# Four plain experts instead of five in the first token group, and six half-units of forms made inside the block-product stage

## The chip, the cores and the metric

One core of a Trainium2 chip runs the whole program. TensorE (PE; PEld is its weight load) multiplies, VectorE (DVE), ScalarE (ACT) and GpSimd (POOL) do the elementwise work, SyncE (SP) issues the DMAs. The metric is device microseconds of one execution.

## The reference

Three layers follow each other. Local attention: 4 batches, 8 heads, 576 positions, head size 64, causal with a window of 64. Then a feed-forward layer (below "first mixture stage") with an ELU on 2304 tokens, 512 to 2048 to 512. Then a dense mixture of eight experts, each 512 to 1024 to 512 with a ReLU, weighted by a matrix P that eight Sinkhorn rounds make from gate logits:

```
h = x @ w_in;  g = where(h > 0, h, exp(min(h, 0)) - 1);  x = g @ w_out
P = exp(x @ w_gate - max);  8 times: P /= P.sum(1); P /= P.sum(0); P *= N / E
for e in range(8):
    h = maximum(x @ w1[e], 0.0)
    out += P[:, e:e + 1] * (h @ w2[e])
```

Nearly all the time is in the matrix products. Each float32 operand is held as a rounded high part and the rest, and a product is three matmuls (high x high, high x rest, rest x high).

## The kernel before

The tokens of the experts are cut into three groups of 768 (NG2 = 3). The experts are computed in two ways.

**Plain** (e_in, e_out): the first group is done as two blocks of 512 and 256 tokens. A unit of this stage is half an expert, four chunks of 128 hidden columns; a chunk is 12 matmuls into a hidden tile (lines 886 to 888), ReLU and split, then matmuls into the outputs (lines 904 to 906). Its weights lie in SBUF as "forms". Experts 0 to KP-1 = 4 are done so for the first group.

**Block product** (l1, l2): an expert on 768 tokens is cut 2 x 2 in each dimension, and seven products take the place of eight. A period (g, e, pp) is half an expert on group g. It has 14 calls of l1 (six matmuls each on 384 columns, line 1080), two per step of the outer loop, and seven calls of l2 (line 1225 in the first group, 18 matmuls on 256 columns; line 1160 in the others, 12 on 384). l2 runs eight steps behind l1, so the first eight steps of the stage have one call of l2 among them. In l1 the accumulator "la" takes four products one on another; between them ACT copies its state out ("a", "u", "v", line 1100), and TensorE must not write it again before. DVE forms c11, c22, c21 and the sums s1 to s4; ACT and DVE or POOL split them into the hidden operands h (lines 1053, 1058, 1062). Experts KP to 7 of the first group and all experts of the other two groups are done so: 6 + 16 + 16 = 38 periods. The weights come from DRAM, where the forms of all eight experts were stored: w1_load puts 256 KB into one of NW1 = 12 buffers, w2_load 512 KB into one of seven. Each w1_load stands 12 calls ahead of its use.

**Forms.** A half-unit is one quarter of an expert's w1 or w2: h = e*8 + p*2 + m, m = 0 for w1 and 1 for w2. Four loads of 128 KB bring it in, POOL makes four sums, ACT rounds the eight pieces (copies), DVE takes the rest (subtractions), and seven pieces of 256 KB go to DRAM. Two pieces of code do it:

- p_tasks, in the last unit of the first mixture stage and through the plain stage, in the order of the list "order" and at the times of a list "due" (12 clocks per plain unit). It has three load buffers, and the forms lie in eight slots, from which the plain stage also uses them.
- q_tasks (lines 771 to 824), for the first N1 half-units of the list "others" (experts 7, 6, ..., KP), in the middle units of the first mixture stage. It has one load buffer "qw", where the sums are made in place, and two form buffers "qf" that go straight to DRAM. It returns ten tasks: load, two empty ones, copies, subtractions with their stores (a store stands on SP behind the subtraction), sums, copies, and so on.

The order on each engine is the order of the code; nothing reorders it. All these DMAs go through SP in that order.

Of the kernel before, what the change touches and what calls it, by code (L numbers as in the profile page):

```python
# [8 lines left out]
F32 = mybir.dt.float32  # L9
R32 = mybir.dt.float32r  # L10
# [8 lines left out]
def kernel(  # L19
# [660 lines left out]

    KP, N1, N3 = 5, 9, 7
    others = [e * 2 * NP + i for e in reversed(range(KP, E)) for i in range(2 * NP)]
    order = [(h, (i + N3) % 2) for i, h in enumerate(others[N1:N1 + N3])]
    NPRE = N3 + 2
    rest = others[N1 + N3:]
    for u in range(2 * KP):
# [1 line left out]
        if u >= 2 and rest:  # L690
            hs.insert(1, (rest.pop(0), hs[3][1]))
        order += hs
    assert sorted([h for h, _ in order] + others[:N1]) == list(range(E * NP * 2))
    rws, sws, forms = {}, {}, {}
    pools = {}

# [67 lines left out]

    def q_tasks(h):
        e, p, m = p_at(h)
        st = {}
        pos = ({2: 0, 0: 1, 3: 2, 1: 3}, {0: 0, 2: 1, 3: 2, 1: 3})[m]  # L770
        to = wd1[e][p] if m == 0 else wd2[e][p // 2][:, :, p % 2]
        hf, hd = FF // 2, DM // 2

        def load():
            rw = st["rw"] = pools["pre"].tile([P, 4, HB2], F32, tag="qw", bufs=1, name="qw")
            for (f, d), s in PURE[m].items():
                f0 = f * hf + p * P
                o = rw[:, pos[s]]
                if m == 0:
                    nc.sync.dma_start(  # L780
                        out=o.rearrange("p (c f) -> p c f", c=2),
                        in_=w1[e][d * hd:(d + 1) * hd, f0:f0 + P].rearrange(
                            "(c p) f -> p c f", p=P
                        ),
                    )
                else:
                    nc.sync.dma_start(out=o, in_=w2[e][f0:f0 + P, d * hd:(d + 1) * hd])

        def high(a, n):
            t = st[a] = pools["pre"].tile([P, 2, 2, HB2], R32, tag="qf", bufs=2, name="qf")  # L790
            nc.scalar.activation(t[:, :n, 0, :], st["rw"][:, a % 4:a % 4 + n], AF.Copy)

        def low(a, n):
            t = st[a]
            nc.vector.tensor_tensor(
                out=t[:, :n, 1, :], in0=st["rw"][:, a % 4:a % 4 + n], in1=r(t[:, :n, 0, :]),
                op=ALU.subtract,
            )
            if a >= 4:
                nc.sync.dma_start(out=to[:, a - 1:a + 1], in_=r(t))  # L800
            else:
                for i in range(n):
                    s = [s for s in pos if pos[s] == a + i][0]
                    nc.sync.dma_start(out=to[:, s], in_=r(t[:, i]))

        def sums():
            rw = st["rw"]
            ops = (
                ((0, 2, 0, ALU.add), (2, 1, 2, ALU.subtract), (1, 0, 1, ALU.subtract),
                 (3, 3, 1, ALU.subtract)),  # L810
                ((0, 2, 0, ALU.subtract), (2, 1, 2, ALU.subtract), (1, 0, 1, ALU.subtract),
                 (3, 3, 1, ALU.add)),
            )[m]
            for o, a, b, op in ops:
                nc.gpsimd.tensor_tensor(out=rw[:, o], in0=rw[:, a], in1=rw[:, b], op=op)

        def nothing():
            pass

        return [  # L820
            load, *[nothing] * 2, lambda: high(0, 2), lambda: (low(0, 2), high(3, 1)),
            lambda: low(3, 1), sums, lambda: high(4, 2),
            lambda: (low(4, 2), high(6, 2)), lambda: low(6, 2),
        ]

# [424 lines left out]
    with tc.manual_schedule():  # L1250
# [152 lines left out]
        for s, st in enumerate(steps):  # L1403
# [16 lines left out]
            if (u, su) == (1, 2):  # L1420
                pre_cm, pools["pre"] = pool("pre")
                qtasks = [f for h in others[:N1] for f in q_tasks(h)]
            elif u < NU - 1 and (u, su) > (1, 2):
                for _ in range(min(2 + su % 2, len(qtasks))):
                    qtasks.pop(0)()
            if u == NU - 1:
                if su == 0:
# [3 lines left out]
                if su == 2:  # L1431
                    assert not bg
                    close(wa_cm)
                    close(raw_cm)
                    open_pool("rw", "right")
                    open_pool("A1", "right")
                    for n in range(3):
                        p_load(n)
                    ptasks += [f for n in range(len(order)) for f in p_tasks(n)]
                elif su > 2:  # L1440
                    while ntask < min(5 * NPRE + 3, 3.0 * (su - 2)):
                        ptasks.pop(0)()
                        ntask += 1
            if extra:
# [72 lines left out]
        ps_cm.__exit__(None, None, None)  # L1517
        for nm in ("w2p", "hp", "tp", "pb"):
            P2[nm + "_cm"], P2[nm] = pool(nm)
        ps2_cm, P2["ps2"] = pool("ps2", space=PSUM)  # L1520
        nw2 = 0
        for s in range(NPD * 7 + LAG):
            k, j = divmod(s, 7)
            if k < NPD:
                for z, (p, pi) in enumerate(pairs[j]):
# [3 lines left out]
                    for f in fs:  # L1529
                        f()  # L1530
                    w1_load(s * 2 + z + NW1)
            if s == LAG - 3:
                l2(0, 0)
            elif s > LAG:
# [10 lines left out]
            for k2 in (k, k + 1, k + 2, k + 3):  # L1545
                if k >= 0 and 0 < k2 < NPD and periods[k2][0] != periods[k2 - 1][0]:
                    slot = 7 * (k - k2 + 2) + j
                    if slot == -7:
                        x_load(periods[k2][0])
                    x_plan(slot)  # L1550
                    if slot == 16:
# [43 lines left out]
```

## Time and profile before

| | us |
|---|---|
| median of 3 runs | 1970.4 (1970.08 to 1970.88) |
| profiled execution, its own time | 1974.2 |
| its span, first to last instruction | 1972.4 |
| PE busy | 1954.1 |
| DVE busy | 1494.2 |
| ACT busy | 858.4 |
| POOL busy | 726.1 |

By the timeline the attention and the first mixture stage reach to about 502 us, the plain stage from there to about 847, the block stage from there to the end. Matmuls are pipelined, so a matmul's own duration is longer than the distance to the next; how long a piece of the program takes is read from the distance of two starts. A table of windows gives each engine's busy time in each stretch. The DMA share counts the 16 DMA engines; since packets can overlap in one engine it can exceed 1.

### The profile page before, as it was taken

Reading aid. Unit: us, or ns where it says so; the run is one execution under the profiler, and the core shown is the slowest. Engines: PE = TensorE matmul, PEld = TensorE weight load, DVE = VectorE, ACT = ScalarE, POOL = GpSimd, SP = SyncE. Lnnn points to the kernel's source line nnn. Section 1 sums busy time; section 2 is a strip of 40 time slices with the busy share of each in tenths; the row PEclk is TensorE's granted clock in tenths of the full one; section 3 lists DMA queues with packets and bytes.
Section 4 is the critical chain, followed back from the end, with each engine's and each line's share of the span. In section 5 each row is a group of like instructions: output and inputs, shape, how many; then the busy total and the mean of one; then the engine's idle time right before and its main releaser. Section 6 shows DMA issues by size and latency. Waiting matters only on the chain.

```text
span 1972.4 us, 33582 instructions
## 1 busy us (share of the span) xinstructions
PE 1954.1 (99%) x11856; PEld 1816.9 (92%) x11856; DVE 1494.2 (76%) x2534; ACT 858.4 (44%) x1801; POOL 726.1 (37%) x723
## 2 busy tenths in 40 slices
PE   8999999999999999999999999999999999999999
PEld 6788888898878888899999999999999999999998
DVE  6746676767698656567787888888888888888886
ACT  8875555555543444333343333333334333333332
POOL 5423232332355554342342323323343323333232
PEclk9999999999999999999999999999999999999999
DMA  9851354467699999868878888888887887888884
GB/s 212 165 110 52 100 173 151 154 210 275 213 381 374 374 366 365 314 234 284 263 242 305 260 261 257 255 266 262 291 260 250 270 266 259 260 260 262 238 279 121
DMA packets 307640, 487.84 MB, mean 247 GB/s; under 512 B 79872, under 2 KB 161936, under 8 KB 303632
## 3 DMA queue, kind: packets, MB, share of 16 engines
q1 hardware_dynamic: 306288, 485.39, 76.3%
q8 instruction: 95, 1.56, 0.3%
q14 instruction: 73, 0.60, 0.1%
q10 hardware_dynamic: 1184, 0.30, 0.1%
HBM read 354.44 MB, written 126.95 MB: 244 GB/s over the span
## 4 chain that ended last, share of the span: by engine, by line
PE 90%; DVE 4%; DMA 2%; ACT 2%; SPq 1%; issue 1%; POOL 0%; ACTq 0%; DVEq 0%; POOLq 0%
PE la L1080 15%; PE ob L1160 11%; PE oa L1160 11%; PE lb L1080 11%; PE p L204 3%; PE ac L538 3%; PE p L206 3%; PE ac L540 3%; PE p L205 2%; PE ac L539 2%; PE ac L904 2%; PE ac L905 2%; PE ac L906 2%; PE p L886 2%; PE p L888 2%; PE p L887 2%
## 5 line engine op out<-in xcount | busy, mean ns | idle before, releaser
L1062 POOL TENSOR_TENSOR h<-s,h 128x384 fp32r<-128x384 f32 x304 | 352.6, 1175 | 721.1 <-ACT h L1053 680.2
L1080 PE MATMUL la<-xf,w1f 128*128 128x384 f32 x1824 | 360.0, 335 | 1.9 <-ACT u L1100 1.3
L1080 PEld LDWEIGHTS la<-xf,w1f 128*128 128x128 f32 x1824 | 318.3, 188 | 3.4 <-ACT u L1100 2.1
L1080 PE MATMUL lb<-xf,w1f 128*128 128x384 f32 x1368 | 273.7, 334 | 0.0
L1053 ACT ACTIVATE h<-s 128x384 fp32r<-128x384 f32 x304 | 155.1, 522 | 245.7 <-DVE s L1104 238.4
L1160 PE MATMUL oa<-h,w2f 128*128 128x384 f32 x1344 | 252.2, 334 | 0.0
L1160 PE MATMUL ob<-h,w2f 128*128 128x384 f32 x1344 | 252.0, 334 | 0.2 <-DVE acc L1177 0.2
L1080 PEld LDWEIGHTS lb<-xf,w1f 128*128 128x128 f32 x1368 | 239.9, 188 | 0.0
L1160 PEld LDWEIGHTS ob<-h,w2f 128*128 128x128 f32 x1344 | 234.4, 188 | 0.5 <-DVE acc L1177 0.5
L1160 PEld LDWEIGHTS oa<-h,w2f 128*128 128x128 f32 x1344 | 234.4, 188 | 0.1
L1058 DVE SCALAR_TENSOR_TENSOR h<-c,h 128x384 fp32r<-128x384 f32 x228 | 187.6, 833 | 31.9 <-ACT h L1053 31.2
L1053 ACT ACTIVATE h<-c 128x384 fp32r<-128x384 f32 x228 | 119.7, 525 | 173.7 <-DVE c L1090 162.6
L725 POOL TENSOR_TENSOR sw<-rw 128x256 f32<-128x256 f32 x110 | 101.0, 919 | 204.6 <-DVE f L755 127.8
L1090 DVE TENSOR_TENSOR c<-c,pb 128x384 f32<-128x384 f32 x192 | 144.5, 753 | 6.6
L1177 DVE TENSOR_TENSOR acc<-oa,acc 128x768 f32<-128x768 f32 (+1 forms) x114 | 105.0, 924 | 37.4 <-PE oa L1160 37.4
L1177 DVE TENSOR_TENSOR acc<-ob,acc 128x768 f32<-128x768 f32 (+1 forms) x110 | 101.2, 923 | 37.1 <-PE ob L1160 37.1
L1104 DVE SCALAR_TENSOR_TENSOR s<-c,s 128x384 f32<-128x384 f32 x152 | 108.3, 713 | 12.0 <-DMA out_dram<-ost 1.0
L246 ACT ACTIVATE hh<-p 128x512 fp32r<-128x512 f32 (+1 forms) x80 | 39.2, 490 | 171.9 <-PE p L888 171.8
L247 DVE SCALAR_TENSOR_TENSOR hl<-p,hh 128x512 fp32r<-128x512 f32 (+1 forms) x80 | 44.3, 556 | 88.5 <-ACT hh L246 88.5
L886 PE MATMUL p<-xh,f 128*128 128x512 f32 (+1 forms) x320 | 108.4, 339 | 0.0
L887 PE MATMUL p<-xl,f 128*128 128x512 f32 (+1 forms) x320 | 107.6, 336 | 0.0
L888 PE MATMUL p<-xh,f 128*128 128x512 f32 (+1 forms) x320 | 107.5, 336 | 0.0
(175 smaller groups left out, 3907.3 us busy)
## 6 DMA issues: line engine op xcount, KB each, us to landing
w1f<-wdi SPq DMA_DIRECT2D x532, 256.0 KB, 4.0
w2f<-wdo SPq DMA_DIRECT2D x266, 512.0 KB, 4.4
wdo<-f SPq DMA_DIRECT2D x28, 1024.0 KB, 7.7
rw<-in_moe_w_dram SPq DMA_DIRECT2D x220, 128.0 KB, 4.9
wdi<-f SPq DMA_DIRECT2D x27, 1024.0 KB, 7.1
wdo<-f SPq DMA_DIRECT2D x28, 768.0 KB, 5.6
wdi<-f SPq DMA_DIRECT2D x27, 768.0 KB, 5.0
raw<-in_moe_w_in_dram SPq DMA_DIRECT2D x16, 512.0 KB, 4.3
```

Source lines behind the costliest of these rows:

```text
L725: nc.gpsimd.tensor_tensor(out=sw[:, o], in0=a, in1=b, op=op)
L886: nc.tensor.matmul(p1[:, :n], w[:, s, 0, cs], xh, start=(c == 0), stop=False)
L887: nc.tensor.matmul(p1[:, :n], w[:, s, 0, cs], xl, start=False, stop=False)
L888: nc.tensor.matmul(p1[:, :n], w[:, s, 1, cs], xh, start=False, stop=(c == NCC - 1))
L1053: nc.scalar.activation(h[:, 0], src, AF.Relu if relu else AF.Copy)
L1058: nc.vector.scalar_tensor_tensor(h[:, 1], src, 0.0, r(h[:, 0]), op0=ALU.max, op1=ALU.subtract)
L1062: nc.gpsimd.tensor_tensor(out=h[:, 1], in0=src, in1=r(h[:, 0]), op=ALU.subtract)
L1080: nc.tensor.matmul(o, w[:, a, c, :], x[:, b, c, :], start=first and c == 0 and z == 0, stop=last and c == 1 and z == 2, skip_group_check=True,
L1090: nc.vector.tensor_tensor(out=t, in0=t, in1=pb[g, e][:, i], op=ALU.mult)
L1104: nc.vector.scalar_tensor_tensor(d[nm], d[a], 0.0, d[b], op0=ALU.max, op1=op)
L1160: nc.tensor.matmul(o[:, c], w[:, p, b, c * P:(c + 1) * P], hs[p][:, a, :], start=fresh and p == 0 and z == 0, stop=False, skip_group_check ...
L1177: nc.vector.tensor_tensor(out=a, in0=src, in1=a, op=ALU.add)
```

## The change

KP goes from 5 to 4, so expert 4 is done as a block product in all three groups: eight periods in the first group instead of six, 40 in all. N1 goes from 9 to 11 (half-units by q_tasks in the first mixture stage), N3 from 7 to 9 (by p_tasks in its last unit). Six half-units of expert 7, the list "tail", are taken out of "others" and are made by q_tasks inside the block stage, one task after each l1 call from the first on, with three empty tasks behind the load (11 tasks per half-unit, 66 in all) and with buffers in a new pool "late". That pool is closed before the inputs of the second group are loaded.

```
-    KP, N1, N3 = 5, 9, 7
-    others = [e * 2 * NP + i for e in reversed(range(KP, E)) for i in range(2 * NP)]
+    KP, N1, N3 = 4, 11, 9
+    tail = [(E - 1) * 2 * NP + i for i in (2, 3, 4, 6, 5, 7)]
+    others = [
+        h for e in reversed(range(KP, E)) for h in range(e * 2 * NP, (e + 1) * 2 * NP) if h not in tail
+    ]
...
-    def q_tasks(h):
+    def q_tasks(h, pre="pre", gap=2):
...
-            load, *[nothing] * 2, lambda: high(0, 2), lambda: (low(0, 2), high(3, 1)),
+            load, *[nothing] * gap, lambda: high(0, 2), lambda: (low(0, 2), high(3, 1)),
...
-                for _ in range(min(2 + su % 2, len(qtasks))):
+                for _ in range(min(3, len(qtasks))):
...
-                    while ntask < min(5 * NPRE + 3, 3.0 * (su - 2)):
+                    while ntask < min(5 * NPRE + 3, 3.4 * (su - 2)):
...
+        pre_cm, pools["late"] = pool("late")
+        qtasks = [f for h in tail for f in q_tasks(h, "late", 3)]
...
                     w1_load(s * 2 + z + NW1)
+                    if qtasks:
+                        qtasks.pop(0)()
...
                     if slot == -7:
+                        if k2 == 2 * (E - KP):
+                            while qtasks:
+                                qtasks.pop(0)()
+                            close(pre_cm)
                         x_load(periods[k2][0])
```

On SP, at the start of the block stage, before: the loads of block weights (w1f from wdi, w2f from wdo) follow each other.

```order
L1021 DMA w1f<-wdi_1_134 128x512 x6
L1021 DMA w1f<-wdi_2_135 128x512 x2
L1032 DMA w2f<-wdo_0_155 128x1024
L1021 DMA w1f<-wdi_2_135 128x512 x2
L1032 DMA w2f<-wdo_0_155 128x1024
```

The same place now; qw is the tail's load buffer, and "wdi<-qf" are its stores.

```order
L783 DMA qw<-in_moe_w_dram 128x2x128 x4
L1024 DMA w1f<-wdi_1_130 128x512
L1024 DMA w1f<-wdi_2_131 128x512 x2
L1035 DMA w2f<-wdo_0_153 128x1024
L1024 DMA w1f<-wdi_2_131 128x512 x2
L807 DMA wdi_1_142<-qf 128x512 x2
L1035 DMA w2f<-wdo_0_153 128x1024
L1024 DMA w1f<-wdi_2_131 128x512
L807 DMA wdi_1_142<-qf 128x512
```

Four loads and the stores have come between the weight loads, each in its turn in the one queue.

On ACT, in the first period of the stage, before: the copies of the accumulator (a, u, v, r) and of the hidden operands h.

```order
L1100 ACTIVATE v<-la 128x384
L1100 ACTIVATE a<-la 128x384
L1053 ACTIVATE h_9230<-c_9217 128x384
L1131 ACTIVATE r_9243<-la 128x384
L1053 ACTIVATE h_9259<-s_9245 128x384
L1053 ACTIVATE h_9262<-s_9249 128x384
L1053 ACTIVATE h_9282<-s_9247 128x384
L1053 ACTIVATE h_9285<-c_9267 128x384
L1100 ACTIVATE u<-la 128x384
```

The same place now; line 794 is the rounding of the tail's forms.

```order
L1103 ACTIVATE v<-la 128x384
L794 ACTIVATE qf<-qw 128x2x256
L1103 ACTIVATE a<-la 128x384
L1056 ACTIVATE h_8716<-c_8701 128x384
L794 ACTIVATE qf<-qw 128x256
L1134 ACTIVATE r_8734<-la 128x384
L1056 ACTIVATE h_8752<-s_8736 128x384
L1056 ACTIVATE h_8755<-s_8740 128x384
L1056 ACTIVATE h_8779<-s_8738 128x384
L1056 ACTIVATE h_8782<-c_8764 128x384
L794 ACTIVATE qf<-qw 128x2x256
L1103 ACTIVATE u<-la 128x384
```

The third rounding of a half-unit, which needs POOL's sums and a free form buffer, now stands right ahead of the copy "u".

On POOL the tail's four sums stand between the subtractions of the hidden operands, which before followed each other:

```order
L1065 TENSOR_TENSOR h_8752<-s_8736,h_8752 128x384
L1065 TENSOR_TENSOR h_8755<-s_8740,h_8755 128x384
L818 TENSOR_TENSOR qw<-qw 128x256 x4
L1065 TENSOR_TENSOR h_8779<-s_8738,h_8779 128x384
L1065 TENSOR_TENSOR h_8797<-s_8766,h_8797 128x384
```

Two subtractions stand ahead of them and two of the same expert half behind them.

## Rows read from the trace of the kernel before

**Rows 1.** The page's head and its first part, busy time and share of each engine
```profile
span 1972.4 us, 33582 instructions
PE 1954.1 (99%) x11856; PEld 1816.9 (92%) x11856; DVE 1494.2 (76%) x2534; ACT 858.4 (44%) x1801; POOL 726.1 (37%) x723
```

**Rows 2.** Table of windows: each engine's busy us (instructions), clock, DMA share, GB/s
```profile
200.00:300.00 100.00, 100.00 (x494) 84.96 (x493) 71.62 (x113) 53.17 (x94) 32.00 (x35) 1.00 0.41 136
...
450.00:500.00 50.00, 50.00 (x222) 41.39 (x222) 37.79 (x47) 29.41 (x44) 18.54 (x20) 1.00 0.81 285
...
560.00:600.00 40.00, 38.84 (x202) 32.41 (x201) 38.06 (x80) 16.36 (x21) 20.66 (x27) 1.00 1.05 389
...
847.00:872.00 25.00, 24.49 (x142) 23.37 (x141) 17.34 (x28) 12.06 (x26) 10.42 (x8) 1.00 0.82 283
872.00:902.00 30.00, 30.00 (x215) 30.00 (x214) 21.51 (x42) 10.42 (x23) 9.34 (x8) 1.00 0.89 296
902.00:932.00 30.00, 30.00 (x216) 30.00 (x215) 21.18 (x42) 10.76 (x23) 9.24 (x8) 1.00 0.82 255
950.00:990.00 40.00, 40.00 (x285) 40.00 (x284) 30.92 (x60) 13.72 (x30) 13.49 (x12) 1.00 0.79 236
...
1010.00:1020.00 10.00, 10.00 (x71) 10.00 (x70) 9.93 (x17) 5.70 (x11) 5.98 (x5) 1.00 0.76 236
```

**Rows 3.** Timeline of PE, plain stage: start us, us, instruction; first matmul of two units
```profile
712.75 0.39 PE L886 MATMUL p<-xh,f 128*128 128x512 f32 x1
...
745.79 0.39 PE L886 MATMUL p<-xh,f 128*128 128x512 f32 x1
```

**Rows 4.** Timeline of ACT, block stage, first group: the copies "a"
```profile
848.90 0.49 ACT L1100 ACTIVATE a<-la 128x384 f32<-128x384 f32 x1 [4.73 <-PE la L1080]
854.10 0.49 ACT L1100 ACTIVATE a<-la 128x384 f32<-128x384 f32 x1 [0.55 <-PE la L1080]
...
922.11 0.49 ACT L1100 ACTIVATE a<-la 128x384 f32<-128x384 f32 x1 [1.46 <-PE la L1080]
...
951.74 0.49 ACT L1100 ACTIVATE a<-la 128x384 f32<-128x384 f32 x1 [1.44 <-PE la L1080]
```

**Rows 5.** DMA, 640 to 700 us: packets; queue, share; issues, KB, median us to landing
```profile
DMA packets 14101, 22.69 MB, mean 378 GB/s; under 512 B 922, under 2 KB 8468, under 8 KB 13470
...
q1 hardware_dynamic: 14096, 22.62, 103.6%
...
rw<-in_moe_w_dram SPq DMA_DIRECT2D x39, 128.0 KB, 5.8
...
wdi<-f SPq DMA_DIRECT2D x5, 768.0 KB, 5.4
```

**Rows 6.** DMA, 250 to 450 us, the first mixture stage
```profile
q1 hardware_dynamic: 23785, 33.42, 49.5%
...
wdi<-qf SPq DMA_DIRECT2D x8, 512.0 KB, 3.0
qw<-in_moe_w_dram SPq DMA_DIRECT2D x28, 128.0 KB, 3.8
```

**Rows 7.** Groups by line and shape: the work of nine half-units in q_tasks
```profile
L815 POOL TENSOR_TENSOR qw<-qw 128x256 f32<-128x256 f32 x36 | 27.1, 752 | 67.1 <-DVE qf L795 57.2 <-ACT m L238 8.5
...
L795 DVE TENSOR_TENSOR qf<-qw,qf 128x512 fp32r<-128x512 f32 x27 | 21.1, 798 | 6.8 <-ACT qf L791 6.8
...
L791 ACT ACTIVATE qf<-qw 128x512 fp32r<-128x512 f32 x27 | 16.8, 624 | 11.0 <-DMA wdi<-qf 4.9 <-DMA qw<-in_moe_w_dram 4.6 <-DMA wdo<-qf 1.1
...
L795 DVE TENSOR_TENSOR qf<-qw,qf 128x256 fp32r<-128x256 f32 x9 | 3.8, 420 | 0.0
```

**Rows 8.** Timeline of ACT and PE, start of the second group
```profile
1051.31 0.81 ACT L1175 ACTIVATE acc<-ob 128x768 f32<-128x768 f32 x1 [4.96 <-DMA out_dram<-acc]
...
1052.56 1.31 PE L1080 MATMUL la<-xf,w1f 128*128 128x384 f32 x6 [0.49 <-ACT v L1100]
```

**Rows 9.** Timeline of POOL in one period of the first group
```profile
941.15 1.39 POOL L1062 TENSOR_TENSOR h<-s,h 128x384 fp32r<-128x384 f32 x1 [1.30 <-ACT h L1053]
949.31 2.60 POOL L1062 TENSOR_TENSOR h<-s,h 128x384 fp32r<-128x384 f32 x2 [6.76 <-PE lb L1080]
```

More of the change, by code (lines that the diff above doesn't have):

```diff
@@ L692 @@
         order += hs
-    assert sorted([h for h, _ in order] + others[:N1]) == list(range(E * NP * 2))
+    assert sorted([h for h, _ in order] + others[:N1] + tail) == list(range(E * NP * 2))
     rws, sws, forms = {}, {}, {}
@@ L774, in load @@
         def load():
-            rw = st["rw"] = pools["pre"].tile([P, 4, HB2], F32, tag="qw", bufs=1, name="qw")
+            rw = st["rw"] = pools[pre].tile([P, 4, HB2], F32, tag="qw", bufs=1, name="qw")
             for (f, d), s in PURE[m].items():
@@ L789, in high @@
         def high(a, n):
-            t = st[a] = pools["pre"].tile([P, 2, 2, HB2], R32, tag="qf", bufs=2, name="qf")
+            t = st[a] = pools[pre].tile([P, 2, 2, HB2], R32, tag="qf", bufs=2, name="qf")
             nc.scalar.activation(t[:, :n, 0, :], st["rw"][:, a % 4:a % 4 + n], AF.Copy)
```

## The prediction

> **What bounds the kernel now.** I read the page's head first, then a table of stretches, then the timeline of TensorE in the two stages that the change trades, then the DMA answers of both. TensorE is busy for 1954.1 of 1972.4 us [rows 1] and for the whole of each stretch shown except those near 560 and 850 us, at a granted clock of 1.00 [rows 2]. So the time is a sum of matmul intervals, and an edit pays only if it removes intervals or adds waits. The reader should then see that the second scarce thing is the DMA engines: from 560 to 600 us they move 389 GB/s at a share of 1.05, and from 640 to 700 us 378 GB/s at 103.6%, the highest levels held anywhere for tens of microseconds, while TensorE loses nothing from 600 on [rows 2, 5]. That is the plain-expert stage, in which forms are made and stored. In the block-product stage behind it the share is 0.82, 0.89, 0.82 and 0.79 [rows 2]: below full, but not by much. The change takes work out of the first stage and puts DMA work into the second.
>
> **The gain.** Five plain experts become four. A unit of the plain stage is half an expert: four chunks, each on 512 and on 256 tokens. The same matmul of two successive units starts at 712.75 and at 745.79 us [rows 3], 33.04 us apart, so an expert takes 66.08 us. In its place come two periods of the block product in the first token group. The copy "a" of one unit opens at 922.11 us and that of the next period at 951.74 us [rows 4], so a period takes 29.63 us and two take 59.26. The difference is 66.08 - 59.26 = 6.82 us. The programs agree: 64 matmuls of line 886 less, 252 of line 1225 and 168 of line 1080 more. TensorE is full before and after the places where this is cut and spliced, so I take 6.8 us as removed from the end.
>
> **Forms moved earlier, in the first mixture stage.** Two more half-units are made in its middle units (eleven for nine), and the last unit starts two more (58 tasks for 48). One half-unit by this code costs DVE three subtractions of 798 ns and one of 3.8 us / 9 = 0.42 us, 2.8 us in all, ACT three copies of 624 ns and one of about 0.4 us, 2.3 us, and POOL four of 752 ns, 3.0 us [rows 7]. Over 200 to 300 us DVE is busy 71.6 of 100 us, ACT 53.2, POOL 32.0 and DMA 0.41; over 450 to 500 us DVE has 37.8 of 50 and DMA 0.81 [rows 2]. Two half-units spread over more than 200 us add under 3% to DVE. I count nothing; what hides it is that every step's matmuls are two steps ahead of their use. Should all DVE time of one such half-unit stand on the path, it would be 2.8 us; that is the upper end, and nothing below zero, since no work leaves these engines there.
>
> **The plain stage itself.** Each remaining unit makes the same five half-units as before at the same due times, and seven tasks are due at its start as before (65 - 58, 55 - 48). It stays at its full DMA share but is one expert shorter. Cost nothing; the wait that it could grow is already in these rows.
>
> **The six half-units in the block stage.** This is the term that decides. They are 66 tasks, one behind each of the 14 first-layer calls of a period. The first eight steps have hardly any second-layer matmuls, and the copies "a" of calls 0 and 5 come 848.90 to 854.10 us, 1.04 us per call [rows 4]; 18 calls pass by 872 us. The other 48 take 48 x 29.63 / 14 = 101.6 us, until about 974 us.
>
> Each engine's load first. DVE gets 2.8 us per 11 calls (23.3 us), which is 3.6 us per 30 on top of 21.2 of 30 [rows 2, 7]: 83%. At 1010 to 1020 us DVE is busy 9.93 of 10 us and TensorE still 10.00 [rows 2], so this is covered. ACT has 10.8 of 30 us, and gets 3.0. POOL's four sums take 3.0 us and stand between subtractions that come in bursts with holes of 6.8 us [rows 9]; ACT's copy behind them must wait for the third, up to about 4 us (one subtraction of 1.4 us ahead and three sums of 0.75 [rows 7, 9]). What such a wait costs is seen once: ACT sat 4.96 us behind an output DMA before line 1175, and TensorE then idled 0.49 us [rows 8]. So an ACT wait of up to about 4.5 us is free, since ACT is idle two thirds of this stage and the accumulator that it must copy out is next written one second-layer block later. Longer ones are paid one for one. In the first 24 us there is no such block between, and there I expect most of what is paid.
>
> Now DMA. A half-unit loads 4 x 128 KB and stores 1.75 MB in five DMAs, nine DMAs with 2.36 million bytes. By the first mixture stage's 49.5% of 200 us for 33.42 MB that is 2.96 us of all sixteen engines per MB, and by the plain stage's 103.6% of 60 us for 22.62 MB it is 2.75 [rows 5, 6]: 6.5 to 7.0 us, say 6.75. Add this to the shares of rows 2, against 1.04 as the most that lasts.
> 847 to 872 us: 0.82 x 25 = 20.5, plus 18/11 half-units = 11.0, so 31.5 / 1.04 = 30.3 us of work in 25: 5.3 too much.
> 872 to 902: 26.7 + 8.7 = 35.4 / 1.04 = 34.0 in 30: 4.0.
> 902 to 932: 24.6 + 8.7 = 33.3 / 1.04 = 32.0: 2.0.
> 932 to 974: 0.79 x 42 + 12.2 = 45.4 / 1.04 = 43.6: 1.6.
> Together 12.9 us behind. By bytes it is milder. The new flow is 2.36 MB per 23.3 us = 101 GB/s: 283 + 155 = 438 in the first stretch (1.64 half-units x 2.36 MB / 25 us = 155), 397, 356, and 337 after that. Against 378 GB/s the first is (438 - 378) x 25 / 378 = 4.0 us behind and the second 1.5; from there it recovers. So the queue falls behind by 5.5 to 12.9 us. Part of that is free. Loads of block weights are issued 12 calls ahead, some 25 us. The tail's own loads have four calls, 8.5 us, until their first copy, against 3.8 to 5.8 us to land [rows 5, 6]. The tightest is a form buffer: there are two, a store is issued about 1.7 us after its call, and three calls later (5.3 or 7.4 us) ACT wants the buffer again, while such stores land in 3.0 us at half load and 5.4 us at full load [rows 5, 6]. With the free 4.5 us of ACT, about 5 us of lateness is hidden. What TensorE pays is then 0.5 to 8 us; between these I take the middle, 4 us, since the two measures of the same traffic have equal claim.
>
> SP also gets 9 issues per half-unit between its weight loads, and a store waits there for DVE; the 12-call lead of the weights covers that. The loads for the next group start as before relative to that group, five periods into the stage, after the last task.
>
> **Sum.** -6.8 + 0 + 0 + 4 = -2.8 us. The profiled execution took 1974.2 us with 1.8 us outside its span [rows 1] and would become 1971.4; the median 1970.4 becomes 1967.6 us.
>
> The Trainium skill ("DMA: Bandwidth & Descriptors", Specifications and Where 436 GB/s comes from) gives a fabric ceiling of 435 GB/s and an HBM limit of about 358 GB/s per core. By the first all but the opening stretch would fit, and the sum would be near -6.8 us; by the second the first two stretches are (438 - 358) x 25 / 358 = 5.6 and (397 - 358) x 30 / 358 = 3.3 us behind, 8.9 in all and about 4 paid. The rows stand between: 389 GB/s was held for 40 us, so 358 is not a wall here, and nothing held 435.
>
> **Rivals.**
> A. The queue takes it all: less than 1 us paid, -6.8 us, 1963.6. For it: by bytes the stage recovers from 902 us on, block weights have 25 us of lead, and the plain stage ran at 103.6% without a TensorE gap. The skill's fabric ceiling above speaks for this too. Against: the plain stage has three load buffers and eight form slots, the tail one and two.
> B. Slower: the two form buffers. Once the DMA queue is more than about 5 us late, ACT stands at the tail's copies for stores to land, the accumulator copies "u" and "v" queue behind it, and TensorE stops; SP stands behind the same stores, so that weight loads are not issued either and the queue gets no work done ahead. Then the whole 12.9 us is paid: -6.8 + 12.9 = +6.1, 1976.5. It decides from 5 us of lateness on, which by share is passed in the first 25 us. Against it: lateness that is paid is also time for the queue to catch up.
> C. The earlier forms cost: 2.8 us for a half-unit's DVE time in the mixture stage beside the 4 us of the tail, +0.0, 1970.4. Against: TensorE was full there with DVE at 76%.
>
> **Numbers.** My forecast 0.50, A 0.22, B 0.20, C 0.08. A measurement of this kernel tells 0.2%, 3.9 us, from no change: faster is below 1966.5, slower above 1974.3. The forecast has -6.3 (0.5 us paid) to +1.2 (8 us paid) and its third below a payment of 2.9 us counts as faster: 0.16, with A 0.38. Same: 0.34 of the forecast, C's 0.08 and 0.02 of B, where part of the 12.9 us is hidden: 0.44. Slower: 0.18. The likeliest case by itself spans 1964.1 to 1971.6; the range for eight in ten reaches from 1963.6, which is A, into B up to 1974.5.
>
> **What would show it.** Right: units of 33.0 us in the plain stage, one expert fewer, and first-group periods of 29.6 us after the tail. In the first five periods TensorE idles some 4 us in all, released by ACT's copies "u", "a" or "v", more in the first 25 us than later, and ACT's own longest waits are at line 794 for stores or for POOL. DMA share near 1.04 there. A is right if those idle times stay under 1 us; B if each period of the tail is 2 us or more too long. I am wrong if TensorE idles between 200 and 550 us, where it does not now, or if the wait is on DVE.

## The result, and the profile after

The changed kernel takes 1984.3 us (median of 6 runs, 1983.2 to 1987.9) against 1970.6 us (6 runs, 1970.1 to 1972.0). The ratio is 1.0072, interval 1.0062 to 1.0083: slower by 13.7 us, and outside the predicted range of 1963.6 to 1974.5.

The page's head of the changed kernel, beside [rows 1]:

```profile
span 1983.7 us, 34055 instructions
...
PE 1950.9 (98%) x11940; PEld 1821.0 (92%) x11940; DVE 1538.2 (78%) x2604; ACT 868.8 (44%) x1845; POOL 749.7 (38%) x739
```

TensorE is busy 3.2 us less in a span that is 11.3 us longer. The idle time is new, and the next step is to find its stretches. Three marks that exist in both kernels do it: the last 24 score matmuls of the attention stage (line 354), the first copy "a" of the block stage, and the copy "a" that opens the second group. [Rows 4] has the second mark of before, at 848.90; the timelines of PE and ACT of before give the other two:

```profile
151.94 0.89 PE L354 MATMUL s<-qkT 64*64 64x128 f32 x24
...
1011.01 0.49 ACT L1100 ACTIVATE a<-la 128x384 f32<-128x384 f32 x1
```

and the same timelines of the changed kernel, with two more period starts (line numbers behind the edit are three higher than before: 1083 is l1, 1103 the copies "a", "u", "v", 794 and 798 the tail's copies and subtractions, 818 its sums):

```profile
149.12 0.89 PE L354 MATMUL s<-qkT 64*64 64x128 f32 x24
...
791.01 0.49 ACT L1103 ACTIVATE a<-la 128x384 f32<-128x384 f32 x1 [4.73 <-PE la L1083]
...
963.08 0.49 ACT L1103 ACTIVATE a<-la 128x384 f32<-128x384 f32 x1 [1.45 <-PE la L1083]
992.72 0.49 ACT L1103 ACTIVATE a<-la 128x384 f32<-128x384 f32 x1 [1.46 <-PE la L1083]
1022.35 0.49 ACT L1103 ACTIVATE a<-la 128x384 f32<-128x384 f32 x1
```

Read them as distances. From the attention mark to the block stage it was 848.90 - 151.94 = 696.96 us and is 791.01 - 149.12 = 641.89: 55.07 less, where two units, 66.08, were cut. So **11.0 us are lost ahead of the block stage**. Its first group took 162.11 us for six periods, so 162.11 + 59.26 = 221.37 for eight, and takes 231.34: **10.0 us are lost there**. Then -6.8 + 11.0 + 10.0 = +14.2 us, against 13.7 measured. (The spans differ by 2.9 us less than that, nearly all of it because before's profiled execution was 151.94 - 149.12 = 2.8 us late already at the attention mark, which no part of the change touches.)

Where it is lost ahead of the block stage, the timeline of PEld shows (idle time before an instruction in brackets), and the table of waits of PE from 200 to 550 us shows for whom TensorE stood:

```profile
299.15 0.19 PEld L538 LDWEIGHTS ac<-gh,w1h 128*128 128x128 f32 x1 [3.05 <-issue]
...
382.51 0.19 PEld L538 LDWEIGHTS ac<-gh,w1h 128*128 128x128 f32 x1 [1.13 <-issue]
...
403.26 0.19 PEld L538 LDWEIGHTS ac<-gh,w1h 128*128 128x128 f32 x1 [2.69 <-issue]
```
```profile
PE ac L538 <- DVE acc L500: 6.1, 3, 2.9
```

With three smaller ones at 410 to 414 us these make 8.4 us; with three more, each under 0.3 us, PEld idles 9.0 us there. In before the only idle times of PEld from 200 to 550 us are 0.35 and 0.22 us, at 546. The stall at 299 us is followed backwards through four engines. POOL, ACT, DVE and PE of the changed kernel, in that order:

```profile
290.20 1.29 POOL L180 TENSOR_TENSOR w1l<-t,w1h 128x512 fp32r<-128x512 f32 x1
291.45 3.63 POOL L818 TENSOR_TENSOR qw<-qw 128x256 f32<-128x256 f32 x4
...
294.30 0.63 ACT L794 ACTIVATE qf<-qw 128x512 fp32r<-128x512 f32 x1 [3.69 <-POOL qw L818]
...
295.66 0.37 ACT L238 ACTIVATE m<-p 128x256 f32<-128x256 f32 x1
...
294.96 0.69 DVE L798 TENSOR_TENSOR qf<-qw,qf 128x512 fp32r<-128x512 f32 x1 [2.92 <-ACT qf L794]
...
297.75 0.68 DVE L798 TENSOR_TENSOR qf<-qw,qf 128x512 fp32r<-128x512 f32 x1
298.35 2.48 DVE L500 TENSOR_TENSOR acc<-ac,acc 128x512 f32<-128x512 f32 x4
...
299.18 0.36 PE L538 MATMUL ac<-gh,w1h 128*128 128x256 f32 x1 [2.88 <-DVE acc L500]
```

POOL splits a weight of the step and only then makes the half-unit's sums. ACT has a copy of these sums next in its order and stands 3.69 us; the step's own work (line 238, the ELU) is behind it. DVE has the subtraction next and stands 2.92 us; behind it are the subtractions and the sums that empty the accumulator (line 500), and TensorE waits 2.88 us for these. No engine is short of time there; each stands in front of work that it could do.

In the block stage the idle times of PEld lie in the first 45 us: 1.88, 3.24, 0.36, 1.04 and 1.73 us, then 0.67 at 898 us, 8.9 us in all, where before had 1.5. The largest, in the timelines of POOL, ACT and PE of the changed kernel, with the call ahead of it for comparison:

```profile
802.20 3.65 POOL L818 TENSOR_TENSOR qw<-qw 128x256 f32<-128x256 f32 x4
...
805.07 0.63 ACT L794 ACTIVATE qf<-qw 128x512 fp32r<-128x512 f32 x1 [2.67 <-POOL qw L818]
805.61 0.47 ACT L1103 ACTIVATE u<-la 128x384 f32<-128x384 f32 x1
...
799.13 1.20 PE L1083 MATMUL la<-xf,w1f 128*128 128x384 f32 x6
...
806.13 2.29 PE L1083 MATMUL la<-xf,w1f 128*128 128x384 f32 x6 [2.92 <-ACT u L1103]
```

The copy "u" comes right behind the tail's copy, and TensorE with it. The same call then lasts 2.29 us instead of 1.20. The table of windows says why, beside [rows 2] (behind the five engines stand PEclk and the DMA share):

```profile
789.00:814.00 25.00, 20.52 (x107) 19.73 (x106) 13.62 (x23) 9.68 (x21) 7.72 (x8) 0.86 0.82 278
...
804.00:814.00 10.00, 7.87 (x36) 7.87 (x37) 4.47 (x8) 3.69 (x8) 3.61 (x5) 0.66 0.91 334
...
844.00:874.00 30.00, 30.00 (x214) 30.00 (x213) 25.29 (x48) 12.60 (x27) 17.15 (x18) 1.00 1.04 395
```

A granted clock of 0.66 over 10 us is 6.8 us at 1.2 GHz (2 x 0.34 x 10), so 3.4 us of matmul time more. The last row is as telling: a whole period with the DMA engines at 1.04 and TensorE without a gap.

### The profile page after: what moved, and what is told of

The parts are those of the page before. It is cut to its first block, busy times and chain, and to the rows that moved or that the text cites. A ratio compares the mean times of both kernels' runs of the same rounds, so it can differ in the third digit from the quotient of the medians.

```text
span 1983.7 us, 34055 instructions
## 1 busy us (share of the span) xinstructions
PE 1950.9 (98%) x11940; PEld 1821.0 (92%) x11940; DVE 1538.2 (78%) x2604; ACT 868.8 (44%) x1845; POOL 749.7 (38%) x739
## 4 chain that ended last, share of the span: by engine, by line
PE 81%; DVE 7%; DMA 4%; ACT 4%; issue 2%; POOL 1%; SPq 1%; DVEq 0%; ACTq 0%; POOLq 0%
PE la L1083 15%; PE lb L1083 11%; PE ob L1163 11%; PE oa L1163 11%; PE ob L1228 3%; PE oa L1228 2%; PE p L889 2%; PE p L890 2%; PE p L891 2%; PE ac L907 2%; PE ac L908 2%; PE ac L909 2%; PE p L204 1%; PE p L205 1%; PE p L206 1%
## 5 line engine op out<-in xcount | busy, mean ns | idle before, releaser
L1065 POOL TENSOR_TENSOR h<-s,h 128x384 fp32r<-128x384 f32 x320 | 371.0, 1175 | 741.8 <-ACT h L1056 716.0
L1083 PE MATMUL la<-xf,w1f 128*128 128x384 f32 x1920 | 380.1, 335 | 5.5 <-ACT u L1103 4.7
L1083 PEld LDWEIGHTS la<-xf,w1f 128*128 128x128 f32 x1920 | 335.3, 188 | 7.3 <-ACT u L1103 5.6
L1083 PE MATMUL lb<-xf,w1f 128*128 128x384 f32 x1440 | 288.4, 334 | 3.1 <-DVE c L1097 3.1
L1083 PEld LDWEIGHTS lb<-xf,w1f 128*128 128x128 f32 x1440 | 252.3, 188 | 3.6 <-DVE c L1097 3.6
L728 POOL TENSOR_TENSOR sw<-rw 128x256 f32<-128x256 f32 x94 | 85.8, 913 | 159.1 <-DVE f L758 98.7
L1103 ACT ACTIVATE v<-la 128x384 f32<-128x384 f32 x80 | 39.3, 491 | 156.1 <-PE la L1083 156.0
L538 PE MATMUL ac<-gh,w1h 128*128 128x512 f32 (+1 forms) x240 | 89.7, 374 | 6.7 <-DVE acc L500 6.1
L227 DVE SCALAR_TENSOR_TENSOR m<-m,p 128x512 f32<-128x512 f32 (+1 forms) x78 | 50.0, 641 | 55.4 <-ACT m L239 55.0
L1107 DVE SCALAR_TENSOR_TENSOR s<-c,r 128x384 f32<-128x384 f32 x160 | 84.5, 568 | 8.1 <-ACT r L1134 5.0
```

What stands on the lines that cost most here:

```text
L227: nc.vector.scalar_tensor_tensor(m, m, -1.0, p1[:, :n], op0=ALU.add, op1=ALU.max)
L538: nc.tensor.matmul(d, wh[:, wc], gh[:, :n], start=f, stop=False)
L728: nc.gpsimd.tensor_tensor(out=sw[:, o], in0=a, in1=b, op=op)
L1065: nc.gpsimd.tensor_tensor(out=h[:, 1], in0=src, in1=r(h[:, 0]), op=ALU.subtract)
L1083: nc.tensor.matmul(o, w[:, a, c, :], x[:, b, c, :], start=first and c == 0 and z == 0, stop=last and c == 1 and z == 2, skip_group_check=True,
L1107: nc.vector.scalar_tensor_tensor(d[nm], d[a], 0.0, d[b], op0=ALU.max, op1=op)
```

## The experiments

Two questions: are the two losses there one without the other, and what makes each? The table sets the losses as above, in us, beside the measured difference from before. "Marks" are the three marks of each profiled execution, "first" is the loss in the stretch ahead of the block stage, "second" that in its first group. "Measured" compares medians, and a single profiled execution can lie off its median: that of e2 is 4.0 us above it. The names e1 to e11 are used from here on.

| kernel | marks | gain | first | second | sum | measured |
|---|---|---|---|---|---|---|
| the change | 149.12, 791.01, 1022.35 | -6.8 | 11.0 | 10.0 | +14.2 | +13.7 |
| e1_mix_alone | 148.51, 855.37, 1017.51 | 0 | 9.9 | 0.0 | +9.9 | +10.2 |
| e2_pace | 148.87, 809.49, 1041.08 | -6.8 | 29.7 | 10.2 | +33.1 | +29.8 |
| e5_lock | 148.22, 779.82, 1010.06 | -6.8 | 0.7 | 8.9 | +2.8 | +3.5 |
| e3_late_tail | 150.98, 791.84, 1022.89 | -6.8 | 10.0 | 9.7 | +12.9 | +14.8 |
| e4_sum_gap | 148.09, 789.33, 1024.31 | -6.8 | 10.4 | 13.6 | +17.2 | +16.2 |
| e6_prefetch | 148.52, 789.82, 1022.39 | -6.8 | 10.4 | 11.2 | +14.8 | +15.2 |
| e7_no_sums | 148.45, 789.88, 1018.87 | -6.8 | 10.6 | 7.6 | +11.4 | +12.9 |
| e8_both | 148.45, 781.20, 1012.28 | -6.8 | 1.9 | 9.7 | +4.8 | +5.4 |
| e11_three_forms | 149.66, 781.40, 1010.54 | -6.8 | 0.9 | 7.8 | +1.8 | +2.1 |
| e9_spaced_late | 148.74, 780.05, 1004.05 | -6.8 | 0.4 | 2.6 | -3.8 | -3.7 |
| e10_spaced | 149.43, 781.74, 1010.78 | -6.8 | 1.4 | 7.7 | +2.3 | +2.1 |

**The mixture stage alone (e1).** In the kernel before:

```diff
-    KP, N1, N3 = 5, 9, 7
+    KP, N1, N3 = 5, 11, 7
-                for _ in range(min(2 + su % 2, len(qtasks))):
+                for _ in range(min(3, len(qtasks))):
```


> The kernel before (five plain experts, no forms in the block stage) with one part of the change alone: eleven half-units instead of nine in the middle units of the first mixture stage, at three tasks per step instead of three and two in turn. In the changed kernel the block stage begins 57.9 us earlier where 66.1 was cut, and TensorE idles 8.4 us between 299 and 415 us. Theory (the pace of these tasks makes those waits): 6 to 9 us slower than before, 1976.5 to 1980, the idle times again at the short steps of 256 tokens. Rival (the 8 us belong to the last unit's faster start or to the plain stage): within 1.5 us of before. My prediction's step (nothing): 1970.6.

1980.6 against 1970.4 us, 1.0053 (1.0038 to 1.0068): +10.2 us with no block-stage tail and no expert less, above the expected 6 to 9. PEld of this run stands at the same places:

```profile
298.05 0.19 PEld L538 LDWEIGHTS ac<-gh,w1h 128*128 128x128 f32 x1 [2.54 <-issue]
380.48 0.19 PEld L538 LDWEIGHTS ac<-gh,w1h 128*128 128x128 f32 x1 [1.24 <-issue]
401.23 0.19 PEld L538 LDWEIGHTS ac<-gh,w1h 128*128 128x128 f32 x1 [2.72 <-issue]
```

So the eleven half-units at their new pace in the middle units make the first loss, without the rest of the change. Whether it is their number or their pace this run does not tell.

**Fewer tasks in the short steps, more in the long ones (e2).** In the changed kernel:

```diff
-                for _ in range(min(3, len(qtasks))):
+                for _ in range(min(1 if j == len(blocks) - 1 else 3 + su % 2, len(qtasks))):
```


> The changed kernel with another pace of the same eleven half-units in the first mixture stage: one task in a step of 256 tokens, four and three in turn in the steps of 512 (110 tasks in the same steps). Theory A (the loss there comes from three tasks in the short steps, 2.8 us of matmuls each): TensorE's idle time between 200 and 420 us falls from 8.4 to 2 us or less, 1976 to 1979. Theory B (it comes from POOL's sums and ACT's copies that wait for them standing in one step, whatever its length): no better than the change, 1983 to 1987.

2000.2 us, 1.0154 (1.0139 to 1.0169): 16 us worse than the change, outside both expected ranges. Taking tasks out of the short steps and putting them into the long ones is no cure. That the short steps have a part in it is not excluded: both long stalls of the change, at 299 and 403 us, come where the ELU behind the tail's copy is one of 256 tokens (the 128x256 of line 238 above).

**The same work, put in other steps (e5).** A half-unit in a cycle of three steps: its load; then both first copies with their subtractions and the sums; then the last copies and subtractions. So nothing on ACT or DVE stands behind the sums of its own step. The short steps of the first of the two middle units get no task; those of the second keep theirs.

```diff
-                qtasks = [f for h in others[:N1] for f in q_tasks(h)]
+                qtasks = [f for h in others[:N1] for f in q_tasks(h, gap=0)]
...
-                for _ in range(min(3, len(qtasks))):
-                    qtasks.pop(0)()
+                if not (u == 1 and j == len(blocks) - 1):
+                    for _ in range(min((1, 4, 3)[nq % 3], len(qtasks))):
+                        qtasks.pop(0)()
+                    nq += 1
```


> The changed kernel with the eleven half-units of the first mixture stage cut in a fixed way over three steps: the load alone; then both first copies, their subtractions and POOL's sums; then the last copies and subtractions, a full step behind the sums (no tasks in the short steps of the first of these units). Theory B of the earlier run (what costs is a step in which POOL's sums, ACT's copy behind them and DVE's subtraction behind that stand together): TensorE's idle time from 200 to 420 us falls from 8.4 to 3 us or less, 5 to 9 us faster than the change, 1975 to 1979. Rival (eleven half-units are too much work for DVE and ACT in these steps, however they are placed): 1982 to 1988.

1973.8 us, 1.0018 (1.0009 to 1.0028): 10.5 us better than the change, with the same instructions. One idle time of 0.69 us is left in the stretch, and the loss ahead of the block stage is 0.7 us. The first loss is a matter of placement, not of load.

**The tail later (e3).** Tasks from call 10 on, gap 2 instead of 3:

```diff
-                    if qtasks:
+                    if qtasks and s * 2 + z >= 10:
```


> The changed kernel with the six half-units of the block stage begun ten calls later, behind the first second-layer call, and with two empty tasks behind a load instead of three so that they end in time. Theory A (the loss of 10 us in the first eight periods is made in the first eight steps, where calls follow each other in 1.04 us, and TensorE's clock drops to its lower level for 6.8 us behind the stalls): 5 to 8 us faster than the change, 1976 to 1979, clock 1.00 throughout the first 25 us of the stage. Theory B (the DMA queue is late, as in my prediction): the same traffic in fewer calls, so as slow as the change or slower, 1984 or more, with ACT's copies waiting for stores.

1985.1 us, 1.0073 (1.0058 to 1.0088): no gain. The stalls of the start are smaller and a new one stands later, because with two empty tasks ACT's copy comes before the load has landed. So this run moves the start and shortens the load's lead in one. ACT, then PEld of this run:

```profile
854.82 0.63 ACT L794 ACTIVATE qf<-qw 128x512 fp32r<-128x512 f32 x1 [6.35 <-DMA qw<-in_moe_w_dram]
855.36 0.47 ACT L1134 ACTIVATE r<-la 128x384 f32<-128x384 f32 x1
...
861.81 1.74 PEld L1083 LDWEIGHTS lb<-xf,w1f 128*128 128x128 f32 x6 [3.93 <-DVE c L1097]
```

**A place between the sums and the copy that reads them (e4).** Gap 2, and one empty task behind "sums":

```diff
-            lambda: low(3, 1), sums, lambda: high(4, 2),
+            lambda: low(3, 1), sums, *[nothing] * (pre == "late"), lambda: high(4, 2),
```


> The changed kernel with one of the three empty tasks of a half-unit in the block stage moved from behind the load to between POOL's sums and the ACT copy that needs them; start and number of tasks as in the change. Theory A (ACT waits for POOL's sums with the accumulator copy u behind it: 2.67 us at 802 us, then 3.24 us of TensorE idle and the lower clock): 4 to 7 us faster than the change, 1977 to 1980. Theory B (DMA late): the load has one call less to land, so ACT waits longer for it, and the time is the same or up to 3 us slower.

1986.5 us, 1.0077 (1.0060 to 1.0093): no gain, and 13.6 us lost in the stage instead of 10.0. PEld still stands 4.13 us at 817 us for "u" and 2.50 at 848 us for DVE; ACT waits 15.8 us for loads, where it was 6.9 in the change. That is what theory B expected.

**Loads one half-unit ahead (e6).** Two buffers "qw" in the tail; the next half-unit's load stands first, then two empty tasks and this one's seven others:

```diff
-            rw = st["rw"] = pools[pre].tile([P, 4, HB2], F32, tag="qw", bufs=1, name="qw")
+            rw = st["rw"] = pools[pre].tile(
+                [P, 4, HB2], F32, tag="qw", bufs=2 if pre == "late" else 1, name="qw"
+            )
```


> The changed kernel with two load buffers in the block stage, and each half-unit's load issued while the one before it is worked on, ten calls ahead of its first copy; all other work as in the change. Theory A (ACT's waits for the tail's loads, up to 6 us long with three or four calls of lead, stall the copies u, v, r and by them DVE and TensorE): 3 to 6 us faster than the change, 1978 to 1981, no ACT wait on a load. Theory B (DMA engines full, so everything is late): the same bytes, the same time as the change, waits moved to the stores. Theory C (POOL's sums and DVE's longer subtractions): within 2 us of the change.

1985.5 us, 1.0078 (1.0059 to 1.0097): no gain. ACT waits no more for loads, and now stands for the stores of a form buffer. The waits of ACT from 778 to 930 us (us in total, times, longest), then ACT and PE in this run, whose lines are two higher again:

```profile
ACT qf L796 <- DMA wdi<-qf: 12.8, 4, 4.9
...
ACT qf L796 <- DMA wdo<-qf: 9.0, 5, 4.0
```
```profile
810.88 0.63 ACT L796 ACTIVATE qf<-qw 128x512 fp32r<-128x512 f32 x1 [4.86 <-DMA wdi<-qf]
...
812.24 0.61 ACT L796 ACTIVATE qf<-qw 128x512 fp32r<-128x512 f32 x1
812.76 0.47 ACT L1105 ACTIVATE a<-la 128x384 f32<-128x384 f32 x1
...
813.28 2.29 PE L1085 MATMUL la<-xf,w1f 128*128 128x384 f32 x6 [5.08 <-ACT a L1105]
```

Two tail copies stand ahead of "a", and the first of them waits for a store. The waits moved to the stores, as theory B had it; whether full DMA engines are the reason is decided by e9 below.

**No sums in the block stage (e7).** This kernel leaves POOL's sums out there, so its forms are not the right ones; only its time is of use.

```diff
-            for o, a, b, op in ops:
+            for o, a, b, op in ops if pre == "pre" else ():
```


> The changed kernel without POOL's four sums of each half-unit in the block stage, so that four of the seven pieces of these six half-units are stored without them; loads, copies, subtractions and stores are as many as before. Theory C (POOL's 18 us, which ACT waits for and which slow DVE's subtractions where they meet): 4 to 8 us faster than the change, 1976 to 1980. Theory A (loads) or B (DMA full): within 2 us of the change, 1982 to 1986.

1983.2 us, 1.0066 (1.0048 to 1.0083): about 1 us better than the change, by the marks 2.4 us in the stage. ACT's waits for stores become 11.8 and 9.3 us.

**The three-step cycle of e5 and the loads ahead of e6 together (e8).**


> The changed kernel with both: the fixed three-step pace in the first mixture stage and the loads ahead in the block stage. If both theories hold and add up: 1969 to 1975, that is 8 to 14 us faster than the change and about as fast as the kernel before. If the two stages do not add up (what is saved early is given back in the block stage): no faster than the better of the two alone.

1975.7 us, 1.0030 (1.0021 to 1.0040): no better than the cycle alone, and just outside the first of the expected ranges.

**A third form buffer in the tail, with the cycle (e11).**

```diff
-            t = st[a] = pools[pre].tile([P, 2, 2, HB2], R32, tag="qf", bufs=2, name="qf")
+            t = st[a] = pools[pre].tile(
+                [P, 2, 2, HB2], R32, tag="qf", bufs=3 if pre == "late" else 2, name="qf"
+            )
```


> The changed kernel with the fixed pace in the first mixture stage and a third form buffer in the block stage, the tasks there as in the change. Theory D: waits for stores go, those for loads and sums stay; 2 to 5 us faster than e5's 1973.8, 1969 to 1972. Theory B (DMA engines full): as e5.

1972.8 us, 1.0008 (0.9999 to 1.0017): 1.0 us below the cycle alone, short of the expected 2 to 5, and the intervals of the two overlap. Waits for stores fall to 0.9 us; waits for the sums are 9.8 us in 5, and PEld stands 2.18 and 3.25 us at 793 and 797 us.

**Everything at once, and off the start (e9).** The cycle, two buffers "qw", and a tail whose tasks are spread: the next load between sums and copy, empty tasks between uses of a buffer, the first copy at call 10.

```diff
-        qtasks = [f for h in tail for f in q_tasks(h, "late", 3)]
+        ts = [q_tasks(h, "late", 0) for h in tail]
+        idle = [lambda: None]
+        qtasks = ts[0][:1] + idle * 9
+        for i, (_, h0, h3, l3, sums, h4, h6, l6) in enumerate(ts):
+            both = lambda a=l3, b=sums: (a(), b())
+            ahead = ts[i + 1][:1] if i + 1 < len(ts) else idle
+            qtasks += [h0, h3, both] + ahead + idle + [h4, h6, l6] + idle * 2
```


> The changed kernel with the fixed pace in the first mixture stage (as in e5) and the block stage's half-units rearranged: loads one half-unit ahead, every store at least four calls ahead of the next use of its form buffer, sums three calls ahead of the copy that needs them, and the first copy only at the tenth call, behind the fast start. Theory D (ACT stands at a form buffer whose store has not landed, 5 to 7 us after its issue, and in the fast start three calls are only 3 us; each earlier run took away one wait and met the next): the stalls go, TensorE idles under 3 us in the first 180 us of the stage: 1965 to 1969, 5 to 9 us faster than e5 and 2 to 5 us faster than before. Theory B (DMA engines full): as slow as e5, 1972 to 1977.

**1967.0 us (11 runs) against 1970.7 (27 runs), 0.9980 (0.9971 to 0.9988): faster than before and than the change.** PEld's idle times over 0.5 us in the first group of the block stage:

```profile
798.86 1.00 PEld L1085 LDWEIGHTS la<-xf,w1f 128*128 128x128 f32 x6 [0.82 <-ACT a L1105]
801.61 2.04 PEld L1085 LDWEIGHTS la<-xf,w1f 128*128 128x128 f32 x12 [0.71 <-ACT u L1105]
836.56 0.99 PEld L1085 LDWEIGHTS la<-xf,w1f 128*128 128x128 f32 x6 [1.02 <-ACT v L1105]
847.03 0.99 PEld L1085 LDWEIGHTS la<-xf,w1f 128*128 128x128 f32 x6 [1.01 <-ACT u L1105]
```

With two smaller ones they make 4.1 us, more than the expected 3, where before had 1.5. The windows of the start and of the first 141 us of the stage:

```profile
779.00:804.00 25.00, 23.91 (x140) 22.91 (x139) 18.46 (x30) 13.87 (x31) 12.48 (x12) 1.00 0.90 312
...
779.00:920.00 141.00, 138.40 (x948) 136.88 (x947) 116.01 (x211) 65.05 (x137) 65.81 (x64) 1.00 1.00 362
```

In the changed kernel the 141 us from the same place, 1 us ahead of the first copy "a", read:

```profile
790.00:931.00 141.00, 133.76 (x897) 132.08 (x896) 110.73 (x200) 61.43 (x130) 61.48 (x61) 0.98 0.96 343
```

The run that stalls less moves more: 362 GB/s against 343. Weight loads land no sooner (w1f: a median of 6.1 us from issue to landing, 6.0 in the change; it was 4.0 in before). Full DMA engines by themselves are not what stops TensorE.

Nor are all waits of ACT gone. In the same 141 us it stands no more for loads or for POOL's sums (6.9 and 6.2 us in the change), but longer for stores, where the change has 6.1 and 4.5 us:

```profile
ACT qf L796 <- DMA wdo<-qf: 10.0, 5, 4.5
ACT qf L796 <- DMA wdi<-qf: 8.7, 8, 3.0
```

What differs is where these waits stand: all of them lie behind the fast start.

**The same with the first copy at call 4 instead of 10 (e10)** (`idle * 3` for `idle * 9`).


> As e9, but with the first copy at the fourth call, inside the fast start. Theory D puts 3 to 6 us on the fast start, where four calls last 4.2 us and a store takes longer to land: 1969 to 1974, with a TensorE stall of 2 to 5 us in the first 25 us of the stage and the lower clock behind it. If the spacing alone is what counts: within 1.5 us of e9.

1972.8 us, 1.0007 (0.9997 to 1.0016): 5.8 us behind e9, 5.0 of it in this stage by the marks. PEld again stands in the start, and the clock falls (0.93 over the first 25 us):

```profile
793.83 1.53 PEld L1085 LDWEIGHTS lb<-xf,w1f 128*128 128x128 f32 x6 [3.08 <-DVE c L1099]
...
809.01 2.04 PEld L1085 LDWEIGHTS la<-xf,w1f 128*128 128x128 f32 x12 [2.75 <-ACT u L1105]
```

## Why the prediction was wrong

**The gain of 6.8 us was right.** The units of the plain stage are still 33.04 us apart and periods after the tail 29.63 us (963.08 to 992.72 to 1022.35). Of the prediction's rivals, A was further off than the forecast; C, at 1970.4, named the mixture stage and not the price; B, at 1976.5, gave the sign, for a reason that holds only in part.

**"I count nothing" for the earlier forms is the step that failed first.** It cost 11.0 us in the change and 10.2 alone. The step summed DVE's work, 2.8 us per half-unit, against a DVE that was busy 71.6 of 100 us [rows 2], and took two steps of lead as cover. Both are facts, and neither is the question. A task is not work to be fitted into free time: it has a fixed place in the order of three engines, and where it waits, all behind it wait. Before, three and two tasks in turn made ten tasks four steps, so each half-unit fell on the same places: the sums and the copy that reads them in one step, the subtraction in the next. At three per step each half-unit stands one task further on than the one before, and in every third of them sums, copy and subtraction share a step. Of these four, the 4th and the 10th (sums at 291 and 396 us) make the two longest stalls; there POOL splits a weight right ahead of the sums. In the 1st and the 7th POOL made the sums early, at 228 and 335 us, and ACT had no wait for them. In the table of waits from 200 to 420 us before has no ACT wait for POOL's sums; the change has:

```profile
ACT qf L794 <- DMA qw<-in_moe_w_dram: 21.7, 8, 4.4
ACT qf L794 <- POOL qw L818: 12.6, 12, 3.7
```

Before's waits for the same loads were 4.6 us [rows 7]. Rival C, which priced this stage at 2.8 us, used the same wrong measure: the work of one half-unit, not the length of a wait. The three-step cycle removes all but 0.7 us of the loss with the work unchanged. The prediction's own test, "wrong if TensorE idles between 200 and 550 us", is what happened.

**The tail: 4 us predicted, 10.0 paid; the waits were found, their cause was not.** ACT does stand at line 794, and "u", "a" and DVE's c behind it, most in the first 25 us, as written: the first period takes 24.80 us, from 791.01 to 815.81, where it took 17.88 in before. But the price was built from DMA lateness, and the 12.9 us of rival B from a queue that could not keep up. The queue that the sum had 5.5 to 12.9 us behind shows in the block weights as 2 us (they land a median of 6.0 us after issue instead of 4.0), against some 25 us of lead. No PE wait for a block weight appears, the period from 844 to 874 us runs at 1.04 without a gap, and e9 moves more with less loss. What stops ACT is one of three waits: the load, sums on POOL, or a store of one of two buffers. Taking away one alone mostly leaves the next. By the marks, a later start with a shorter lead of the load (e3) gave 0.3 us, another place for the sums (e4) and earlier loads (e6) made it worse by 3.6 and 1.2, no sums (e7) gave 2.4, and a third form buffer (e11, against e5) 1.1. All of them spaced, with the first copy as early as in the change, give 2.3 us (e10: 1010.78 - 781.74 = 229.04, so 7.7 are still lost), no more than the sums alone; with the start left free as well it is 7.4 of the 10.0 us (e9).

**"An ACT wait of up to about 4.5 us is free" came from the wrong place.** [Rows 8] show a wait with a second-layer block between the copy and its use. In the first eight steps calls follow each other every 1.04 us [rows 4] with hardly any such block. There the four calls ahead of a load's first copy are 4.2 us, not the 8.5 of the prediction, and the three until a form buffer is used again 3.1 us, not 5.3 to 7.4. I saw that the start is fast, and still priced the stage by its DMA surplus instead of by its waits. e9 against e10 prices this start: 5.8 us, 5.0 by the marks. Behind the start the rule nearly holds: ACT stands 18.7 us for stores in e9, and TensorE loses the 1.02 us at 836.56 and the 1.01 us at 847.03, each behind two waits of ACT in a row (4.50 and 1.30 us the first time); single waits of up to 3.04 us cost it nothing.

**Not in the sum at all: what a stall costs beyond its length.** In the changed kernel TensorE ran 6.8 us at 1.2 GHz behind the 3.24 us stall at 806 us, and 3.4 us at about 300 us (a clock of 0.72 in the window 298 to 304, below), 5.1 us of matmul time in all. Idle time and clock account for the losses: 9.0 + 1.7 = 10.7 of 11.0 ahead of the block stage, and 8.9 - 1.5 + 3.4 = 10.8 against 10.0 in it.

```profile
298.00:304.00 6.00, 4.82 (x26) 4.73 (x27) 3.58 (x7) 0.82 (x3) 0.00 (x0) 0.72 0.60 175
```

**Open.** How the waits for POOL, loads and stores share the loss in the first eight steps is not settled, since each removed wait uncovers another. Nor is it settled how much the later start would give without the spacing. In e3 the largest stall came from the load's shorter lead: 3.93 us, and about 1.7 us for a clock of 0.83 over the 10 us behind it. Without these 5.6 us e3 would lose some 4 us in the stage, by this estimate, and no run has the later start with the full lead. The 2.6 us that e9 still loses are idle time, 4.1 us against before's 1.5, behind the copies "a", "u" and "v".

## What to carry to other kernels

When tasks are spliced into an in-order stream, do not add their work to busy shares: list, step by step, which engine stands at the task for whom, and which instruction of the critical engine's chain is queued right behind it. Keep producer and consumer of a task in different steps, with a lead of a whole buffer turn, and splice nothing where the accumulator's copies have no other block between them. And expect little from removing one wait of such a chain, since the next one takes its place: here it took the spacing and the free start together.

## What the runs showed of the hardware

The granted clock falls to its lower level after short stalls of an otherwise full TensorE: 6.8 us behind 3.24 us of PEld idle in the changed kernel, 0.86 over the first 25 us in the cycle run (stalls 2.39 and 3.25 us), and 1.00 where no stall was over 1.02 us (e9). It is no sharp rule in these rows: behind 2.69 us at 403 us in the changed kernel the clock stayed at 1.00, and behind 2.72 us at 401 us in the mixture-alone run it was 0.81 over 9 us.

DVE's subtractions slow down beside POOL. The same operation in the changed kernel, apart from a POOL instruction and beside two, with these:

```profile
820.75 0.68 DVE L798 TENSOR_TENSOR qf<-qw,qf 128x512 fp32r<-128x512 f32 x1
...
829.29 1.51 DVE L798 TENSOR_TENSOR qf<-qw,qf 128x512 fp32r<-128x512 f32 x1
...
829.02 1.24 POOL L1065 TENSOR_TENSOR h<-s,h 128x384 fp32r<-128x384 f32 x1 [3.98 <-ACT h L1056]
...
830.22 1.46 POOL L1065 TENSOR_TENSOR h<-s,h 128x384 fp32r<-128x384 f32 x1
```

0.68 becomes 1.51 us, and the next subtraction of that size, from 830.73, takes 1.50. Each ends some 0.55 us behind the end of a POOL instruction (830.26 and 831.68), as if it had waited for it, while POOL's own take little longer than usual (1.24 and 1.46 us; line 1065 has a mean of 1.19 from 785 to 932 us). The Trainium skill ("SBUF — State Buffer", SBUF: two separate sides) says that DVE with two SBUF inputs and a GpSimd operation that reads SBUF exclude each other on a shared port pair, one blocked for the other's whole instruction; the trace agrees, with DVE the one that waits here.
